# Retention attention and a top-2 adapter mixture: 64-token steps on 64x64 array tiles, an undecayed state, and a fixed order on every engine

## The chip, the cores and the metric

The kernel runs on one core of a Trainium2 chip. The metric is device time in microseconds (us): the median of the runs of one kernel. A core has a matrix engine (TensorE, PE in the profile; its weight loads are PEld), a vector engine (VectorE, DVE), a scalar engine (ScalarE, ACT), GpSimd (POOL), and SyncE (SP), which here only issues DMAs. Each engine works through its own queue in order; engines wait for one another by semaphores. PE writes to PSUM, which has eight banks; DVE and ACT copy out of PSUM.

## The reference, cut to what matters

```python
# q, k, v: [8 batches, 8 heads, 576 tokens, 64], float32
scores = scale * q @ k.T                       # per batch and head
ret    = scores * gamma[h] ** (i - j)          # for i >= j, else 0
x      = ret @ v                               # as [4608 tokens, 512]
logits = x @ w_gate                            # 8 experts, the best 2 are kept
w      = softmax(the two logits)
out    = x + sum over the two experts of w * ((x @ A[e]) @ B[e])   # rank 16
```

Because the decay is a product, `gamma ** (i - j)`, it can be split into a factor on q and a factor on v. Attention over earlier tokens can then go through a 64x64 state per head, the sum of k times v, instead of through scores.

## The kernel before, in words

The 576 tokens are cut into four blocks of 128 and one of 64. A unit is one block of two sequences (all 8 heads of both); there are 16 full units and 4 units for the last 64 tokens, in the order block by block, 20 in all. Inputs come by quads: four sequences of one block, three DMAs of 1 MB (q, k, v) on SP's queue, three quads of buffers. `issue(t // 2 + 2)` in the main loop asks for the quad that is two ahead.

For a unit t the stages are:

- `stage_T` (L229): PE transposes q and k by 64-row pieces, DVE copies q out while multiplying by the decay (`aqp`), ACT copies k out.
- `stage_S` (L291): scores k x q of 128 by 128 tokens per head, two 64-row tiles of the array side by side; DVE masks them into `rt` (L302).
- `stage_O`: the state's part of the output, `px` (L359), the new state's sum `pu` (L373); DVE adds (L387) and POOL multiplies by `g128`, the decay over 128 tokens (L388).
- `stage_R` (L408): masked scores times v, added in `px`; ACT copies `px` to `xT` (L417).
- `stage_Z` (L447): gate and all A matrices in one matmul per 128 rows, `pz`; then the routing on DVE and ACT (L460 to L479).
- `stage_B` (L512), `stage_X` (L493) and `stage_Y` (L533) of unit t - 1: x transposed back into `po`, the weighted z transposed, times B added in `po`; ACT copies `po` to `osb` (L543) and SP stores it (L548).

`scale_v` multiplies v by its decay on POOL (L197). Each float32 matmul shows as two matmuls and two weight loads in the profile; transposes show as one. The last four units (L341, L426, and the 64*64 form of L291) work on 64 tokens and use 64x64 tiles.

The order of instructions on each engine is set by the Tile framework's scheduler from the order of the code and the dependencies; PSUM comes from a pool of eight one-bank buffers that go around. SP's queue holds all loads and all stores of the kernel.

Of the kernel before, what the change touches and what calls it, by code (L numbers as in the profile page):

```python
# [9 lines left out]
FP32 = mybir.dt.float32  # L11
# [3 lines left out]
AFT = mybir.ActivationFunctionType  # L15


@with_exitstack
def kernel(
# [19 lines left out]
    LH = S - 128 * NFULL  # L39
    QUAD = 4  # L40
    NQ = B // QUAD

    scale = 1.0 / float(np.sqrt(Dh))
    gam = 1.0 - 2.0 ** (-5.0 - np.arange(H, dtype=np.float64))
    jj = np.arange(128, dtype=np.float64)

    ident32_np = np.eye(128, dtype=np.float32)
    tri_np = (jj[None, :] >= jj[:, None]).astype(np.float32)
    j64 = np.arange(128) % 64
    i64 = np.arange(64)  # L50
    trih_np = (i64[None, :] >= j64[:, None]).astype(np.float32)
    aqp_np = np.zeros((128, HP, 128), dtype=np.float32)
    g128_np = np.zeros((128, HP), dtype=np.float32)
    for hp in range(HP):
        for ho in range(2):
            g = gam[2 * hp + ho]
            aqp_np[64 * ho : 64 * ho + 64, hp, :] = scale * g ** jj[None, :]
            g128_np[64 * ho : 64 * ho + 64, hp] = g**128.0
    gv_np = np.stack([gam[h] ** (-jj) for h in range(H)], axis=1).astype(np.float32)
    gvh_np = np.stack([gam[h] ** (-j64.astype(np.float64)) for h in range(H)], axis=1).astype(  # L60
        np.float32
    )
    i64_np = np.concatenate([np.eye(64), np.eye(64)], axis=0).astype(np.float32)
    first_np = i64_np
    rest_np = np.concatenate(
        [ident32_np, tri_np, trih_np, gv_np, gvh_np, g128_np], axis=1
    ).astype(np.float32)
    NPK = rest_np.shape[1]
    dr_first = nc.inline_tensor(first_np, "c_first")
    dr_rest = nc.inline_tensor(rest_np, "c_rest")  # L70
    dr_aqp = nc.inline_tensor(aqp_np, "c_aqp")

    cpool = ctx.enter_context(tc.tile_pool(name="consts", bufs=1))
    iop = ctx.enter_context(tc.tile_pool(name="io", bufs=3))
    wk = ctx.enter_context(tc.tile_pool(name="work", bufs=2))
    mo = ctx.enter_context(tc.tile_pool(name="moe", bufs=3))
    pp = ctx.enter_context(tc.tile_pool(name="pp", bufs=8, space=bass.MemoryType.PSUM))

    id64 = cpool.tile([128, 64], FP32, tag="id64", name="id64")
    nc.sync.dma_start(out=id64, in_=dr_first.ap())  # L80
# [3 lines left out]
    pack = cpool.tile([128, NPK], FP32, tag="pack", name="pack")  # L84
    aqp = cpool.tile([128, HP, 128], FP32, tag="aqp", name="aqp")
    ident32 = pack[:, 0:128]
    tri = pack[:, 128:256]
    trih = pack[:, 256:320]
    gv = pack[:, 320 : 320 + H]
    gvh = pack[:, 320 + H : 320 + 2 * H]  # L90
    g128 = pack[:, 320 + 2 * H : 320 + 2 * H + HP]

    AW = []
    for par in range(2):
        AW.append(cpool.tile([128, HP, ER + E], FP32, tag=f"AW{par}", name=f"AW{par}"))
    Bcat = cpool.tile([128, Dm], FP16, tag="Bcat", name="Bcat")
    ident16 = cpool.tile([128, 128], FP16, tag="ident16", name="ident16")

    def load_moe():
        for dt in range(HP):  # L100
            nc.sync.dma_start(  # L101
                out=AW[0][:, dt, 0:ER].rearrange("p (e r) -> p e r", e=E),
                in_=moe_A[:, 128 * dt : 128 * dt + 128, :].rearrange("e d r -> d e r"),
            )
        nc.sync.dma_start(
            out=AW[0][:, :, ER : ER + E],
            in_=moe_w_gate.rearrange("(t p) e -> p t e", p=128),
        )
        nc.gpsimd.dma_start(out=Bcat, in_=moe_B.rearrange("e r d -> (e r) d"))


    nat = {}

    def issue_full(c, qd, split):
        tiles = []
        for src, tag in ((q, "q32"), (k, "k32"), (v, "v32")):
            tiles.append((src, iop.tile([128, QUAD * H, Dh], FP32, tag=tag, name=tag)))
        parts = ((0, 2), (2, 4)) if split else ((0, 4),)
        for lo, hi in parts:
            for src, tl in tiles:  # L120
                if split and lo == 0 and src is k:
                    nc.sync.dma_start(out=aqp, in_=dr_aqp.ap())
                if split and lo == 0 and src is v:
                    nc.sync.dma_start(out=pack, in_=dr_rest.ap())
                if split and lo == 2 and src is q:
                    load_moe()
                nc.sync.dma_start(  # L127
                    out=tl[:, lo * H : hi * H, :],
                    in_=src[
                        QUAD * qd + lo : QUAD * qd + hi, :, 128 * c : 128 * c + 128, :  # L130
                    ].rearrange("b h j d -> j (b h) d"),
                )
        for half in range(2):
            nat[(c, 2 * qd + half)] = [
                tl[:, half * 2 * H : half * 2 * H + 2 * H, :] for _, tl in tiles
            ]

    def issue_half(qd):

        s0 = 128 * NFULL  # L140
        tiles = []
        for src, tag in ((q, "q32"), (k, "k32"), (v, "v32")):
            tiles.append((src, iop.tile([128, QUAD * H, Dh], FP32, tag=tag, name=tag)))
        for slot in range(2):
            for src, tl in tiles:
                for par in range(2):
                    b = QUAD * qd + 2 * slot + par
                    nc.sync.dma_start(
                        out=tl[64 * par : 64 * par + LH, slot * H : slot * H + H, :],
                        in_=src[b, :, s0 : s0 + LH, :].rearrange("h j d -> j h d"),  # L150
                    )
            nat[(NFULL, 2 * qd + slot)] = [
                tl[:, slot * H : slot * H + H, :] for _, tl in tiles
            ]

    quads = [(c, qd) for c in range(NFULL + 1) for qd in range(NQ)]

    def issue(n):
        if n < len(quads):
            c, qd = quads[n]  # L160
            if c < NFULL:
                issue_full(c, qd, n == 0)
            else:
                issue_half(qd)

    issue(0)

    issue(1)
    nc.vector.tensor_copy(out=ident16, in_=ident32)
    gdec = cpool.tile([128, HP, 2, Dh], FP32, tag="gdec", name="gdec")  # L170
    nc.gpsimd.tensor_copy(
        out=gdec.rearrange("p a b d -> p a (b d)"),
        in_=g128.unsqueeze(2).broadcast_to((128, HP, 2 * Dh)),
    )
    P = [
        cpool.tile([128, HP, 2, Dh], FP32, tag=f"P{bp}", name=f"P{bp}")
        for bp in range(NP)
    ]

    def swap_aw():  # L180
        for ho in range(2):
            nc.gpsimd.tensor_copy(
                out=AW[1][64 * ho : 64 * ho + 64],
                in_=AW[0][64 - 64 * ho : 128 - 64 * ho],
            )

    units = [(c, 2 * qd + s) for c, qd in quads for s in range(2)]
    st = {}

    def scale_v(t):  # L190
        c, bp = units[t]
        full = c < NFULL
        v32 = nat[(c, bp)][2]
        nb = 2 if full else 1
        g = gv if full else gvh
        for b in range(nb):
            nc.gpsimd.tensor_tensor(  # L197
                out=v32[:, b * H : b * H + H, :],
                in0=v32[:, b * H : b * H + H, :],
                in1=g.unsqueeze(2).broadcast_to((128, H, Dh)),  # L200
                op=ALU.mult,
            )

    def stage_T(t):
        c, bp = units[t]
        full = c < NFULL
        q32, k32, v32 = nat[(c, bp)]
        qT = wk.tile([128, HP, 2, 128], FP32, tag="qT", name="qT")
        kT = wk.tile([128, HP, 2, 128], FP32, tag="kT", name="kT")
        L = 128 if full else LH  # L210
        for src, dst, nm in ((q32, qT, "q"), (k32, kT, "k")):
            dv = dst.rearrange("p a b i -> p a (b i)")[:, :, 0 : 2 * L].rearrange(
                "p a (b i) -> p a b i", i=L
            )
            if full:
                ps = [
                    pp.tile([128, HP, 2, 64], FP32, tag="pb", name=f"pt_{nm}")
                    for _ in range(2)
                ]
            else:  # L220
                ps = [
                    pp.tile([128, HP, 64], FP32, tag="pb", name=f"pt_{nm}")
                    for _ in range(2)
                ]
            for hp in range(HP):
                for b in range(2 if full else 1):
                    for r in range(2):
                        sl = slice(64 * r, 64 * r + 64)
                        nc.tensor.matmul(  # L229
# [381 lines left out]
```

## Time and profile before

| | |
|---|---|
| median of 3 runs | 208.59 us (207.39 to 208.97) |
| span of the profiled execution | 205.1 us |
| what lies around the span (median minus span) | 3.5 us |
| busy: PE, PEld, DVE, ACT, POOL | 183.8, 166.2, 108.7, 76.6, 59.6 us |
| granted TensorE clock | 0.995 mean |
| moved by DMA | 39.14 MB, mean 191 GB/s |

The profiled execution has no time of its own beside its span; the 3.5 us are the median of the runs less that span. The page's busy times say how long an engine had something running. The timeline says in which order, and a bracket at the end of a line tells how long the engine was idle before and what ended it. SPq is SP's own queue: a DMA's line there is the time that the issue held the queue, not the time of the transfer.

### The profile page before, as it was taken

The numbers are of one execution on the slowest core, as the hardware profiler recorded it, in microseconds if no ns is written. First come the engines' busy times: TensorE is split into PE (matmuls) and PEld (weight loads), VectorE is DVE, ScalarE is ACT, GpSimd is POOL, SyncE is SP. The second block draws the span as 40 slices with busy tenths as digits, with TensorE's granted clock in tenths as the row PEclk, the third lists the DMA queues.
The fourth block names the chain that finished last, engine by engine and source line by source line (L and its number), as shares of the span: only waits on it lengthen the run. The fifth ranks groups of instructions, "written<-read, shape, count | busy, mean of one in ns | idle before, by whom it ended". The sixth has DMA issues, their size and how long they took to land.

```text
span 205.1 us, 8039 instructions
## 1 busy us (share of the span) xinstructions
PE 183.8 (90%) x3564; PEld 166.2 (81%) x3564; DVE 108.7 (53%) x286; ACT 76.6 (37%) x206; POOL 59.6 (29%) x60
## 2 busy tenths in 40 slices
PE   0476989799999999999999999999999999999950
PEld 0376969598999999999999999999999899888830
DVE  0226364937374746465656565656565655456630
ACT  2022324153525262625252525253434344454430
POOL 1144323521818202727202720643222402000000
PEclk9999999999999999999999999999999999999997
DMA  5989999799998988991799969756545311222222
GB/s 114 277 109 246 249 243 280 194 290 290 253 319 245 261 249 274 284 297 36 220 286 254 266 215 293 213 145 179 150 118 158 96 51 60 101 79 76 58 47 61
DMA packets 57442, 39.14 MB, mean 191 GB/s; under 512 B 30912, under 2 KB 52672, under 8 KB 57408
## 3 DMA queue, kind: packets, MB, share of 16 engines
q1 hardware_dynamic: 57264, 38.50, 68.0%
q8 instruction: 28, 0.46, 0.9%
q0 software_dynamic: 144, 0.13, 0.4%
q14 instruction: 6, 0.05, 0.1%
HBM read 29.32 MB, written 9.44 MB: 189 GB/s over the span
## 4 chain that ended last, share of the span: by engine, by line
PE 72%; SPq 9%; DVE 7%; DMA 5%; ACT 3%; issue 1%; ACTq 0%
PE pz L447 16%; PE px L408 12%; PE ps_s L291 12%; PE pu L373 6%; PE px L359 6%; PE pt_q L229 5%; DMA k<-in_k_dram 5%; PE po L512 4%; SPq L127 4%; PE pt_k L229 4%; PE po L533 3%; DVE rt L302 2%; PE px L426 2%; ACT osb L543 2%; SPq L101 2%; PE pzt L493 2%
## 5 line engine op out<-in xcount | busy, mean ns | idle before, releaser
L197 POOL TENSOR_TENSOR v<-v,pack 128x512 f32<-128x512 f32 x36 | 36.6, 1042 | 28.0 <-DMA v<-in_v_dram 28.0
L417 ACT COPY xT<-px 128x512 f32<-128x512 f32 x32 | 18.7, 585 | 66.0 <-PE px L408 66.0
L388 POOL TENSOR_TENSOR P<-pn,gdec 128x512 f32<-128x512 f32 x16 | 20.3, 1271 | 75.3 <-DVE pn L387 58.9
L302 DVE TENSOR_TENSOR rt<-ps_s,pack 128x512 f32<-128x512 f32 x64 | 39.7, 682 | 4.2 <-PE ps_s L291 4.2
L291 PE MATMUL ps_s<-qT,kT 64*128 64x128 f32 (+1 forms) x640 | 37.4, 275 | 1.2 <-ACT kT L250 1.2
L447 PE MATMUL pz<-AW,xT 128*128 128x136 f32 x288 | 37.8, 283 | 0.4 <-ACT zT L498 0.4
L291 PEld LDWEIGHTS ps_s<-qT,kT 64*128 64x128 f32 (+1 forms) x640 | 33.7, 184 | 5.3 <-DVE lg L460 3.4
L241 DVE TENSOR_TENSOR qT<-pt_q,aqp 128x512 f32<-128x512 f32 x32 | 20.6, 686 | 31.1 <-PE pt_q L229 31.1
L408 PE MATMUL px<-rt,v 128*64 128x128 f32 x512 | 34.1, 275 | 1.8 <-DVE rt L302 1.7
L447 PEld LDWEIGHTS pz<-AW,xT 128*128 128x128 f32 x288 | 34.7, 190 | 0.6 <-ACT zT L498 0.5
L543 ACT COPY osb<-po 128x256 f32<-128x256 f32 x72 | 23.1, 375 | 25.8 <-PE po L533 25.8
L408 PEld LDWEIGHTS px<-rt,v 128*64 128x64 f32 x512 | 29.0, 137 | 3.8 <-DVE rt L302 2.5
L250 ACT COPY kT<-pt_k 128x512 f32<-128x512 f32 x32 | 17.2, 589 | 19.2 <-PE pt_k L229 19.2
L460 DVE COPY lg<-pz 128x16 f32<-128x16 f32 (+1 forms) x20 | 3.5, 173 | 35.0 <-PE pz L447 35.0
L229 PE MATMUL pt_q<-id,q 64*128 64x64 f32 x288 | 13.6, 234 | 6.7 <-DMA q<-in_q_dram 6.7
L373 PE MATMUL pu<-v,k 128*64 128x64 f32 x512 | 18.9, 225 | 0.0
L373 PEld LDWEIGHTS pu<-v,k 128*64 128x64 f32 x512 | 16.5, 137 | 2.7 <-issue 2.1
L229 PEld LDWEIGHTS pt_q<-id,q 64*128 64x128 f32 x288 | 10.8, 142 | 9.6 <-issue 9.4
L229 PE MATMUL pt_k<-id,k 64*128 64x64 f32 x288 | 12.8, 228 | 3.4 <-DMA k<-in_k_dram 3.4
L473 DVE SCALAR_TENSOR_TENSOR cm<-lg,m,sg 128x8 f32<-128x8 f32 x36 | 9.9, 294 | 8.8 <-ACT sg L468 8.8
L229 PEld LDWEIGHTS pt_k<-id,k 64*128 64x128 f32 x288 | 10.9, 143 | 3.8 <-issue 1.7
L359 PE MATMUL px<-qT,P 64*64 64x128 f32 x384 | 13.2, 275 | 0.0
(34 smaller groups left out, 139.9 us busy)
## 6 DMA issues: line engine op xcount, KB each, us to landing
out_dram<-osb SPq DMA_DIRECT2D x32, 256.0 KB, 3.2
q<-in_q_dram SPq DMA_DIRECT2D x2, 512.0 KB, 5.0
k<-in_k_dram SPq DMA_DIRECT2D x2, 512.0 KB, 6.0
v<-in_v_dram SPq DMA_DIRECT2D x2, 512.0 KB, 5.4
q<-in_q_dram SPq DMA_DIRECT2D x8, 128.0 KB, 3.4
k<-in_k_dram SPq DMA_DIRECT2D x8, 128.0 KB, 3.3
v<-in_v_dram SPq DMA_DIRECT2D x8, 128.0 KB, 4.1
out_dram<-osb SPq DMA_DIRECT2D x8, 128.0 KB, 2.4
```

The costliest lines, as they stand in the source:

```text
L197: nc.gpsimd.tensor_tensor(out=v32[:, b * H : b * H + H, :], in0=v32[:, b * H : b * H + H, :], in1=g.unsqueeze(2).broadcast_to((128, H, Dh) ...
L229: nc.tensor.matmul(ps[r][:, hp, b, :] if full else ps[r][:, hp, :], lhsT=src[sl, b * H + 2 * hp : b * H + 2 * hp + 2, :], rhs=id64[sl, :], ...
L241: nc.vector.tensor_tensor(out=o, in0=ps[r], in1=aqp[:, :, 64 * r : 64 * r + 64] .unsqueeze(2) .broadcast_to((128, HP, 2, 64)), op=ALU.mult,)
L291: nc.tensor.matmul(o, lhsT=kT[sl, hp, b, :], rhs=qT[sl, hp, b, :], start=(a == 0 and (b == 0 or not full)), stop=True, skip_group_check=True,)
L302: nc.vector.tensor_tensor(out=r.rearrange("p a b i -> p (a b) i"), in0=ps[ho].rearrange("p a b i -> p (a b) i"), in1=tri.unsqueeze(1).broa ...
L359: nc.tensor.matmul(px[b][64 * cc : 64 * cc + 64, hp, :], lhsT=P[bp][64 * ho : 64 * ho + 64, hp, b, :], rhs=qT[64 * ho : 64 * ho + 64, hp, ...
L373: nc.tensor.matmul(pu[64 * ho : 64 * ho + 64, hp, b, :], lhsT=s["k"][:, b * H + h, :], rhs=s["v"][:, b * H + h, :], start=(hp == 0 and b = ...
L388: nc.gpsimd.tensor_tensor(out=pf, in0=pn, in1=gdec.rearrange("p a b d -> p (a b d)"), op=ALU.mult,)
L408: nc.tensor.matmul(px[b][64 * cc : 64 * cc + 64, hp, :], lhsT=s["v"][:, b * H + h, :], rhs=rt[h][:, b, :], start=(c == 0 and hp == 0), sto ...
L417: nc.scalar.copy(out=xt, in_=px[b])
L447: nc.tensor.matmul(pz[:, b, :], lhsT=xts[b][:, dt, :], rhs=AW[b][:, dt, :], start=(dt == 0), stop=(dt == HP - 1), skip_group_check=True,)
L543: nc.scalar.copy(out=osb[:, b, :, cc ^ b, :], in_=po[cc][:, b])
```

## The change

All attention goes in steps of 64 tokens. A unit is still 128 rows of two sequences, but the 128 rows are two steps g = 0, 1 of 64 tokens (for the last 64 tokens: two pairs of sequences, so there are 2 such units in place of 4, and 18 units in all). Scores, state products, state sums and scores times v are all 64x64x64 matmuls on the four 64x64 tiles of the array, so the upper right 64 by 64 part of each 128 by 128 block of scores is not computed, and there are more and smaller matmuls. q and v are multiplied by the whole decay from the sequence's start (`gq`, `gv`, by position) on POOL before they are used, so the state is a plain sum: two DVE adds for each unit, no decay of the state. ACT copies both transposes out of PSUM.

`tc.manual_schedule()` keeps the order of the code on every engine. Banks are named by hand. The code keeps the two row tiles of the array from writing into one bank at once: where the state products change over, PE's next matmul waits for a NOP on SP's queue, which itself waits for PE's last matmul (`end_turn`, `begin_turn`). Two changeovers come in each row of the main loop. Stores are issued at the end of a row, two rows after the unit's attention. Inputs have four quads of buffers instead of three. The constants come in one small DMA; A and the gate come by 12 DMAs on SP's queue instead of 5, B by 4 on POOL's instead of 1.

The core of the diff (the new side; the old functions stand above):

```diff
+    def scale(t, which, eng):
+        c, _ = units[t]
+        x = nat[units[t]][0 if which == "q" else 2].rearrange("p (s h) d -> p s h d", s=2)
+        tab = gq if which == "q" else gv
+        for s in range(2):
+            eng.tensor_tensor(out=x[:, s], in0=x[:, s],
+                in1=tab[:, c, :].unsqueeze(2).broadcast_to((128, H, Dh)), op=ALU.mult)
...
+    def bankA(r):
+        return (2, 3) if r % 2 == 0 else (6, 7)
...
+    def pe_S(t):
+        ps = [bank(ho, [128, HP, 2, 64], name=f"ps_s{ho}") for ho in range(2)]
+        for hp in range(HP):
+            for s in range(2):
+                for ho in range(2):
+                    for g in range(2):
+                        nc.tensor.matmul(
+                            ps[ho][half(g), hp, s, :],
+                            lhsT=kT[half(ho), g, hp, s, :],
+                            rhs=qT[half(ho), g, hp, s, :],
...
+    def end_turn(ins):
+        n = nc.sync.nop(nofuse=True)
+        tc.add_manual_dep(n.ins, ins.ins.name, SYNC, reason="row tile's last write")
+        turn.append(n)
+
+    def begin_turn(ins):
+        if turn:
+            tc.add_manual_dep(ins.ins, turn.pop().ins.name, SYNC, reason="other row tile's bank")
+
+    def pe_I(t, part):
+        for a in range(HP // 2):
+            for s in range(2):
+                for par in range(2):
+                    g = part ^ par
+                    P = state_of(t, s, g)
+                    if P is None:
+                        continue
+                    hp = 2 * a + par
+                    for ho in range(2):
+                        c = ho ^ par
+                        ins = nc.tensor.matmul(
+                            px[g][half(c), hp, s, :],
+                            lhsT=P[0][half(ho), hp, P[1], :],
+                            rhs=qT[half(ho), g, hp, s, :],
...
+                        begin_turn(ins)
+        end_turn(ins)
...
+    def pe_U(t, part):
+        for hp in range(2 * part, 2 * part + 2):
+            for s in range(2):
+                for g in range(2):
+                    for ho in range(2):
+                        h = s * H + 2 * hp + ho
+                        nc.tensor.matmul(pu[g][half(ho), hp, s, :],
+                            lhsT=k32[half(g), h, :], rhs=v32[half(g), h, :], ...
...
+    def ev_U(t):
+        if P0 is None:
+            nc.vector.tensor_copy(out=f(Pm), in_=f(pu[0]))
+        else:
+            nc.vector.tensor_tensor(out=f(Pm), in0=f(pu[0]), in1=f(P0), op=ALU.add)
+        nc.vector.tensor_tensor(out=f(Pn), in0=f(pu[1]), in1=f(Pm), op=ALU.add)
...
+    def pe_R(t):
+        for hp in range(HP):
+            for s in range(2):
+                for g in range(2):
+                    for ho in range(2):
+                        c = ho ^ (hp & 1)
+                        ins = nc.tensor.matmul(px[g][half(c), hp, s, :],
+                            lhsT=v32[half(g), s * H + 2 * hp + ho, :],
+                            rhs=rt[ho][half(g), hp, s, :], ...
+                        begin_turn(ins)
...
+    for r in range(NU + 2):
+        if r % 2 == 0:
+            issue(r // 2 + 2)
+        if r + 2 < NU:
+            scale(r + 2, "q", nc.gpsimd)
+            scale(r + 2, "v", nc.gpsimd)
+        if r + 1 < NU:
+            pe_T(r + 1, "q")
+            ev_T(r + 1, "q")
+            pe_T(r + 1, "k")
+        if 0 <= r - 2:
+            pe_B(r - 2)
+        free = bankA(r + 1)
+        if 0 <= r - 2:
+            pe_pzt(r - 2, free[0])
+        if r + 1 < NU:
+            ev_T(r + 1, "k")
+        if 0 <= r - 1 < NU:
+            pe_Z(r - 1, free[1])
+            route1(r - 1)
+        if 0 <= r - 2:
+            pe_Y(r - 2)
+            ev_Y(r - 2)
+        if 0 <= r - 1 < NU:
+            route_sig(r - 1)
+        if r < NU:
+            pe_S(r)
+            ev_S(r)
+            alloc_x(r)
+            pe_I(r, 0)
+            pe_U(r + 1, 0)
+            pe_I(r, 1)
+            pe_U(r + 1, 1)
+        if 0 <= r - 1 < NU:
+            route2(r - 1)
+        if r < NU:
+            ev_U(r + 1)
+            pe_R(r)
+            ev_x(r)
+        if 0 <= r - 2:
+            store(r - 2)
```

Before this loop the new code calls `issue(0)` (a quad in halves, with the weights' DMAs between them) and `issue(1)`, and transposes unit 0 and sums its state (`pe_T(0, ...)`, `pe_U(0, ...)`). `pe_T`, `pe_B`, `pe_pzt`, `pe_Z`, `route1`, `route2`, `pe_Y` do what stages T, B, X, Z and Y did, on the same shapes. The 1 MB loads of a quad have the same access patterns as before.

## The prediction

> **What bounds the kernel now.** I read the page first, then the chain of waits, then the timeline of PE and of SP's queue. The page has PE busy for nine tenths of the span and no other engine above 53%.
>
> ```profile
> PE 183.8 (90%) x3564; PEld 166.2 (81%) x3564; DVE 108.7 (53%) x286; ACT 76.6 (37%) x206; POOL 59.6 (29%) x60
> PEclk9999999999999999999999999999999999999997
> DMA  5989999799998988991799969756545311222222
> ```
>
> From about 51 us the chain is PE alone and repeats every 10.05 us, once a unit. PE's timeline of one unit (start, length):
>
> ```profile
> 103.36 2.07 PE L447 MATMUL pz<-AW,xT 128*128 128x136 f32 x16
> 105.27 0.60 PE L533 MATMUL po<-Bcat,zT 128*128 128x256 f16 x4
> 105.80 2.06 PE L291 MATMUL ps_s<-qT,kT 64*128 64x128 f32 x32
> 107.78 1.10 PE L359 MATMUL px<-qT,P 64*64 64x128 f32 x32
> 108.81 1.15 PE L373 MATMUL pu<-v,k 128*64 128x64 f32 x32
> 109.80 1.92 PE L408 MATMUL px<-rt,v 128*64 128x128 f32 x32
> 111.65 0.52 PE L229 MATMUL pt_q<-id,q 64*128 64x64 f32 x10
> ```
>
> Groups overlap at their ends, so I take starts less starts. The chain of waits has the same pieces without the overlap: pt_q 0.64, pt_k 0.49, po 0.49, pzt and its gap 0.22, pz 1.91, po 0.44 (together 4.19), scores 1.99, state products 1.03, state sums 1.08, scores times v 1.75: 10.04 us.
>
> The start is another stage. In 41.8 us PE finishes only three units (some 31 us of work) because inputs arrive slowly, and SP's own queue shows how: one 1 MB load holds it for as long as the data ahead of it needs to drain.
>
> ```profile
> 29.11 3.54 SPq L127 DMA_DIRECT2D q<-in_q_dram  x1
> 33.11 4.74 SPq L127 DMA_DIRECT2D k<-in_k_dram  x1
> 38.30 3.52 SPq L127 DMA_DIRECT2D v<-in_v_dram  x1
> 41.92 3.69 SPq L548 DMA_DIRECT2D out_dram<-osb  x1
> ```
>
> Later, with DMAs quiet beforehand, two stores and a quad still hold the queue from 97.26 to 107.59, **10.3 us**:
>
> ```profile
> 97.26 0.93 SPq L548 DMA_DIRECT2D out_dram<-osb  x2
> 98.40 0.72 SPq L127 DMA_DIRECT2D q<-in_q_dram  x1
> 99.58 3.50 SPq L127 DMA_DIRECT2D k<-in_k_dram  x1
> 103.54 4.05 SPq L127 DMA_DIRECT2D v<-in_v_dram  x1
> ```
>
> Today nobody but the DMAs themselves waits for that queue. After the change PE does.
>
> **The change, part by part: matmuls.** The price of a 64x64x64 matmul is in the last units, which have that shape now:
>
> ```profile
> 181.69 0.69 PE L291 MATMUL ps_s<-qT,kT 64*64 64x64 f32 x32
> 182.20 1.11 PE L341 MATMUL pq<-qT,P 64*64 64x64 f32 x32
> 183.39 1.12 PE L426 MATMUL px<-rh,v 64*64 64x64 f32 x32
> ```
>
> L291 uses all four tiles in turn: 182.20 less 181.69 is 0.51 us for 32 records, 16 ns each. L426 also uses four; once its inputs are there its records go four every 58 ns, 14.6 each. L341 visits only two tiles and pays 32. In the new code scores, state products, sums and scores times v each visit four tiles in turn and have 64 records a unit, so each costs 64 x 15.5 = 1.0 us (0.94 to 1.02; 2.0 if state products behaved like L341). A row costs 4.19 + 4.0 = **8.2 us** for 10.04: 1.0 saved on scores, 0.75 on scores times v, 0.1 on sums, nothing on state products. The 4.19 stay, shapes being the same. There are 18 rows for 20 units.
>
> The Trainium skill, "TensorE: Matmul & The Clock Gate", section "Wait — 56ns, not 53.3ns?", has a floor of about 25 ns between starts, however small the matmul. That speaks against this change: 256 records would be 6.4 us for 4.0, and a row would be longer than today's. The 14.6 and 16 ns rows say the floor does not hold across tiles, and I go by them.
>
> **Other engines.** DVE loses the q copies (20.6 + 3.0 us) and nearly half of the mask (64 to 36 of 682 ns, 19 us) and gains 16 state adds of 0.69 (11 us): about 77 for 108.7 us. ACT gains the q copies, 36 x 0.585 = 21 us, and has about 6.1 us in a row of 8.2. POOL has 70 products of 1.04, 4.2 us a row. These are hidden behind PE. If not, one place shows first: U's first half writes the bank that ACT empties with four osb copies (two take 0.65, so 1.3) after Y, with only scores and half the state products (1.5 us) and 0.2 of handoffs between: 0.2 us late (0 to 0.4), in 8 rows not held otherwise: 1.6 us. Removing POOL's state decay (20.3 us) gains nothing, since PE did not wait for it.
>
> **SP's queue.** The NOPs stand, in program order, behind every DMA issued before them. Moved past or onto that queue: a quad in every even row stands ahead of both its NOPs, a unit's stores behind them.
>
> - *Start.* Row 0 comes after issue(0), issue(1) and issue(2). Before, the third quad's v leaves the queue at 41.8 us. The constants shrink from 458 to 106 KB (1.4 us at 250 GB/s), while the weights cost 12 issues for 5 (5.4 us now; 12 x 0.58, the shortest, is 7.0: 1.6 more if not covered by draining). I take 40.5 us (39 to 42.5) for the first matmul of the second half of row 0's state products. Before, three units were done at that time.
> - *Even rows 4 to 10.* Count from the last state product of the row before. SP sees it 0.3 us later, passes two stores and a quad (10.3), and wakes PE (0.1): 10.7. PE meanwhile has half the sums 0.5, scores times v 1.0, 4.19, scores 1.0, half the products 0.5 and half the sums 0.5, with 0.2 of bank wait: 7.8. PE waits 2.9 us (2.0 to 3.6) four times. Row 2 has no stores ahead: 1.9. Together **13.5**. Rows 12 and 14 load half quads (the first quad's halves held the queue 4.95 us): none.
> - Behind the waiting NOP stand stores and next loads; loads are two rows ahead, osb has four buffers, so nothing waits for those. Behind the waiting matmul stands all of PE.
> - *Handoff.* No row has a PE to SP to PE trip. A semaphore event on SP takes 17 to 28 ns, a matmul 218 from its start to its end: at least 0.25 us, and by DVE to PE handoffs (0.2 to 0.5 idle) at most 0.6. I take 0.45, covered by 0.5 us of sums, except in rows 15 to 17, which have none: twice 0.45 each.
>
> **Start of the clock.** PE's first score group took 3.79 us where the next took 2.06, and the granted clock is down again after the end:
>
> ```profile
> 199.00:202.00 3.00, 0.39 (x2) 0.11 (x2) 0.00 (x0) 0.76 (x3) 0.00 (x0) 1.00 0.55 124
> 202.00:205.00 3.00, 0.00 (x0) 0.00 (x0) 0.00 (x0) 0.00 (x0) 0.00 (x0) 0.65 0.20 46
> ```
>
> The last column but two is the clock; it drops to half at 202.87, 3.3 us after the last matmul. PE idles well over 10 us in row 0, so it restarts at half speed: 1.8 us (3.79 less 2.06, rounded up). The 2.9 us waits are just below 3.3 and I price them at nothing (at most 1.8 each). The same skill page, section "Part 1: The HAM clock gate", gives the idle window as about 3.4 us; by it the sum would be the same.
>
> **The end.** From the last unit's pz to the end are now 9.4 us (195.68 to 205.06). A whole unit adds the px copies 1.35 ahead, 0.75 of pz, 0.65 of routing and transposed z, 0.65 of the other unit's osb copies in front of its sigmoids, 0.65 of its own, 1.1 for four stores: 14.6, with handoffs 15.0.
>
> **Sum:** 40.5 to row 0's second half; 2.0 for the rest of row 0; row 1 7.5 (no B and Y; 0.45 for its first xT); rows 2 to 14 13 x 8.2 = 106.6 and 1.6; rows 15, 16 8.1 each and row 17 7.9 (24.1); waits 13.5; end 15.0; clock 1.8. That is **212.6 us** of span against 205.1. The median before lies 3.5 above its span, so 216.1: PE saves 1.85 us in each full unit and two short units, and SP's queue takes it back, some 18 us at the start (unit 2's scores times v end at 60.1, now at 41.7) and 11.6 in rows 4 to 10.
>
> **Rivals.**
>
> - *PE is not held by SP's queue* (the NOPs pass ahead of loads, so the fixed order isn't what it says). For it: only code order, no row, puts them behind. Against: every store in SP's timeline stands behind loads until they leave. Data then set the start: row 3 cannot begin before the third quad's k, about 43.5. Then 12 x 8.4 = 100.8, 24.1, 15.0: 183.4, **186.9** with 3.5. It decides if two stores and a quad pass in under 7.8 us. 0.14.
> - *Only the start is held.* A quad's issue takes 0.7 per load when the queue has drained (q at 98.40), and pauses of PE may let it. Against it are 3.50 and 4.05 right after. 212.6 less 13.5 plus 3.5: **202.6**. 0.14.
> - *The waits drop the clock.* 2.9 grows past 3.3 and five restarts cost 1.8 each: 216.1 + 9 = **225.1**. 0.13.
> - *State products at 32 ns*, like L341: 1.0 in each of 17 rows, half of it hidden in five: 216.1 + 14 = **230**. Against: four tiles, not two. 0.04.
>
> **Numbers.** My forecast gets 0.55, at 216.1; with the bounds above (start, waits, bank wait, handoffs) 207 to 224. A change under 1% cannot be told from none here. Faster by over 1% (below 206.5): the first rival and most of the second, 0.27. Within 1%: the low end of mine and the rest of the second, 0.07. Slower: 0.66. The range 198 to 228 leaves out the first rival and the top of the last two, under 0.2.
>
> **What would show it.** In the profile after: PE's four attention groups near 1.0 us each, PE's busy time well below 183.8; PE idle from before 30 to about 40 us, ended by SP; in rows 2 to 10 every second state-product group preceded by about 2.9 us of idle ended by SP's queue, the other rows near 8.2. It is wrong if PE's waits end on DVE, ACT or a DMA, if state products in even rows start without a wait, or if a 64x64 group takes over 1.3 us.

## The result and the profile after

The changed kernel takes **271.0 us** (median of 4 runs, 266.66 to 273.95); the kernel before took 207.99 us beside it. The ratio is **1.2908** [1.2792, 1.3023]: 29% slower, where 3.6% (216.1 us) was forecast, and far above the range's 228. Medians are over all runs and ratios over undisturbed ones alone, so the two need not divide to the same figure, and the profiled execution, from which the rows below come, is one of the slower ones. It took 271.86 us, its span is 269.9, its mean granted clock 0.873 (0.995 before).

The page first, with the lines that answer to those shown of the kernel before, then the shares of the chain that ended last and the costliest groups:

```profile
PE 177.7 (66%) x5612; PEld 161.9 (60%) x5612; DVE 77.1 (29%) x197; ACT 91.4 (34%) x236; POOL 74.7 (28%) x81
PEclk9999755799799869985998589977999999899995
DMA  8959999919836990789179807990494197022215
...
q8 instruction: 44, 0.72, 1.2%
...
PE 45%; SPq 36%; issue 12%; DVE 2%; ACT 2%; ACTq 0%
...
L406 PE MATMUL px<-qT,Pm 64*64 64x64 f32 x512 | 26.3, 240 | 27.7 <-SPq L385 26.8
...
L432 PE MATMUL pu<-v,k 64*64 64x64 f32 x1024 | 29.8, 248 | 10.4 <-issue 6.2
...
L466 PE MATMUL px<-rt,v 64*64 64x64 f32 x1152 | 28.0, 247 | 11.1 <-issue 10.2
...
L336 PE MATMUL ps_s<-qT,kT 64*64 64x64 f32 x1152 | 23.4, 228 | 5.2 <-issue 5.2
```

PE was busy 90% of the time and is now busy 66%; the other engines are nowhere near full. PE's idle time has two names. `SPq L385` is the NOP of the handoff, which was forecast. `issue` is time in which PE waited for nothing that the profile shows, and that was not forecast. The clock row, nearly flat before, has holes all along the span. Line q8 looks harmless at 1.2% of the DMA engines, but it is the one that matters: 44 packets of kind "instruction". The page of before has 28:

```profile
q8 instruction: 28, 0.46, 0.9%
```

The chain of waits (start, length) shows the start, one row without an SP wait, an even row with one, and a piece of the odd row behind it:

```profile
43.17 4.29 SPq L139
47.57 1.00 PE px L406 x13
...
64.90 0.72 PE ps_s L336 x34
65.62 2.03 issue
67.65 0.80 PE ps_s L336 x25
...
84.58 3.85 SPq L139
88.89 5.21 SPq L139
94.21 1.13 PE px L406 x32
...
102.93 1.09 PE ps_s L336 x64
104.02 0.48 PE px L406 x31
104.50 0.55 PE pu L432 x30
105.22 1.31 issue
```

PE waits for SP until 47.57, as the third quad's v leaves SP's queue (43.17 plus 4.29). At 102.93 the groups have the price that was forecast: 64 records of scores in 1.09 us, half the state products in 0.48. But then PE stands still for 1.31 us, and at 65.62 in the middle of one scores group for 2.03 us, with its inputs there. The group after that stop, 25 records in 0.80 us, runs at half the pace: the granted clock is at half from 67.96 to 71.37.

SP's queue (start, length) over the same stretch:

```profile
20.96 2.34 SPq L139 DMA_DIRECT2D q<-in_q_dram  x1
...
38.44 4.28 SPq L139 DMA_DIRECT2D k<-in_k_dram  x1
43.17 4.29 SPq L139 DMA_DIRECT2D v<-in_v_dram  x1
71.11 12.08 SPq L319 DMA_DIRECT2D out_dram<-osb  x4
83.42 0.70 SPq L139 DMA_DIRECT2D q<-in_q_dram  x1
84.58 3.85 SPq L139 DMA_DIRECT2D k<-in_k_dram  x1
88.89 5.21 SPq L139 DMA_DIRECT2D v<-in_v_dram  x1
```

The two quads that row 0 has to wait for hold the queue from 20.96 to 47.46, 26.5 us (23.4 before). Ahead of them the 12 loads of A and the gate held it from 6.24 to 16.36, 10.1 us.

**Whose are the stops?** From here on a gap is counted from the start of one matmul to the start of the next, which is some 0.2 us more than the idle time in a profile row. After 50 us PE has 24 gaps of over 1 us. Four end on SP, at 94.21, 120.33, 147.47 and 174.75. The other 20 resume, when all that stands in PE's queue is counted (weight loads, matmuls, and 121 semaphore and drain instructions), at instructions 1217, 1473, 1985, 2753, 3521, 3777, 4289, 5057 and so on to 9665: every difference is a multiple of 256. Each of the 20 ends 1.2 to 1.8 us after a packet of 16,384 bytes on queue q8 has landed; the four on SP end 4.8 us or more after one. PE's 11,224 matmuls and weight loads divided by 256 are 43.8, and 44 packets came; before, 7,128 are 27.8, and 28 came. So a packet holds 256 instructions of 64 bytes, and the theory for the experiments was: **PE runs out of instructions.** In the expectations that theory is called F; Q is the theory of the prediction, that SP's queue holds PE and the rest is cheap.

### The profile page after: what moved, and what is told of

Its sections match the earlier page's. It is cut to its first block, busy times and chain, and to the rows that moved or that the text cites. A ratio compares the mean times of both kernels' runs of the same rounds, so it can differ in the third digit from the quotient of the medians.

```text
span 269.9 us, 12185 instructions
## 1 busy us (share of the span) xinstructions
PE 177.7 (66%) x5612; PEld 161.9 (60%) x5612; DVE 77.1 (29%) x197; ACT 91.4 (34%) x236; POOL 74.7 (28%) x81
## 4 chain that ended last, share of the span: by engine, by line
PE 45%; SPq 36%; issue 12%; DVE 2%; ACT 2%; ACTq 0%
SPq L139 25%; PE pz L240 10%; PE px L466 8%; PE px L406 6%; PE pu L432 5%; PE ps_s L336 5%; SPq L129 3%; PE pt_q L191 3%; SPq L99 3%; PE pt_k L191 3%; PE po L213 2%; SPq L149 2%; PE po L294 2%; SPq L319 2%; DVE rt L350 1%
## 5 line engine op out<-in xcount | busy, mean ns | idle before, releaser
L160 POOL TENSOR_TENSOR q<-q,pack 128x512 f32<-128x512 f32 x34 | 34.7, 1042 | 84.3 <-DMA q<-in_q_dram 70.1
L406 PE MATMUL px<-qT,Pm 64*64 64x64 f32 x512 | 26.3, 240 | 27.7 <-SPq L385 26.8
L406 PEld LDWEIGHTS px<-qT,Pm 64*64 64x64 f32 x512 | 22.1, 151 | 31.3 <-SPq L385 28.0
L432 PE MATMUL pu<-v,k 64*64 64x64 f32 x1024 | 29.8, 248 | 10.4 <-issue 6.2
L466 PE MATMUL px<-rt,v 64*64 64x64 f32 x1152 | 28.0, 247 | 11.1 <-issue 10.2
L466 PEld LDWEIGHTS px<-rt,v 64*64 64x64 f32 x1152 | 24.9, 159 | 12.6 <-issue 12.0
L432 PEld LDWEIGHTS pu<-v,k 64*64 64x64 f32 x1024 | 25.5, 158 | 11.7 <-issue 6.8
L336 PE MATMUL ps_s<-qT,kT 64*64 64x64 f32 x1152 | 23.4, 228 | 5.2 <-issue 5.2
L406 PE MATMUL px<-qT,P 64*64 64x64 f32 x512 | 21.4, 231 | 7.5 <-issue 7.3
L336 PEld LDWEIGHTS ps_s<-qT,kT 64*64 64x64 f32 x1152 | 20.3, 140 | 9.4 <-issue 5.9
L191 PEld LDWEIGHTS pt_q<-pack,q 64*128 64x128 f32 x288 | 12.6, 160 | 19.0 <-DVE q L160 7.6
```

What stands on the lines that cost most here:

```text
L160: eng.tensor_tensor(out=x[:, s], in0=x[:, s], in1=tab[:, c, :].unsqueeze(2).broadcast_to((128, H, Dh)), op=ALU.mult,)
L191: nc.tensor.matmul(ps[g][:, hp, s, :], lhsT=src[half(g), s, 2 * hp : 2 * hp + 2, :], rhs=id64[half(g), :], is_transpose=True, start=True, ...
L336: nc.tensor.matmul(ps[ho][half(g), hp, s, :], lhsT=kT[half(ho), g, hp, s, :], rhs=qT[half(ho), g, hp, s, :], start=True, stop=True, skip_g ...
L406: ins = nc.tensor.matmul(px[g][half(c), hp, s, :], lhsT=P[0][half(ho), hp, P[1], :], rhs=qT[half(ho), g, hp, s, :], start=x_start(t, g, c) ...
L432: nc.tensor.matmul(pu[g][half(ho), hp, s, :], lhsT=k32[half(g), h, :], rhs=v32[half(g), h, :], start=True, stop=True, skip_group_check=True,)
L466: ins = nc.tensor.matmul(px[g][half(c), hp, s, :], lhsT=v32[half(g), s * H + 2 * hp + ho, :], rhs=rt[ho][half(g), hp, s, :], start=x_start ...
```

## The experiments

Eight kernels ran. The first three test F against Q, the next two test single steps of the forecast, the last three ask what in the kernel before could be had.

**The handoff on ScalarE's queue, which holds no DMA.** In the changed kernel:

```diff
-        n = nc.sync.nop(nofuse=True)
+        n = nc.scalar.nop(nofuse=True)
```

> The changed kernel with the two NOPs of each row on ScalarE's queue in place of SyncE's; nothing else differs. Theory Q (SyncE's queue alone holds PE, and the extra time over the forecast is more of the same): no wait on SyncE is left, rows are 8.2 us, and the time is near 187 us, the figure of the first rival in the prediction. Theory F (PE runs out of instructions: it has 11,224 of them against 7,128, and 64x64 matmuls use up 256 in 2 us, faster than the next 256 arrive): the idle of 1.3 to 2.8 us with no releaser ('issue') stays, once every 256 or 512 PE instructions, some 25 times, 2 us each; then 215 to 230 us. Theory C (the clock halves after SyncE's waits and is what makes the rest slow): clock back at 0.99 and no 'issue' idle, near 190 us.

Measured: 254.81 us, 1.2077 [1.1923, 1.2231] times the kernel before; the profiled execution has a span of 248.2 us and a clock of 0.932. PE's waits:

```profile
PE px L466 <- issue: 17.2, 11, 3.4
PE pu L432 <- issue: 8.2, 5, 2.9
...
PE px L406 <- issue: 6.8, 4, 2.6
```

(The columns are us in total, times, longest.) No wait for a handoff is left among them. Of the 29% lost, 8 points went with SP's queue: some 17 of 60 us. Theory Q alone falls, and so does C: the stops are there, and the clock did not come back to 0.99. F is right in kind, and all 20 gaps of over 1 us after 45 us resume at the first instruction of a packet, but its figure of 215 to 230 us was low. The gaps grew to 3.6 us while the loads came earlier; that the loads lengthened them fits the streams below and was not tested here.

**Only the first two quads loaded, and used for all rows,** which makes the DMAs quiet:

```diff
+        if n >= 2:
+            for half in range(2 if c < NFULL else 1):
+                nat[(c, 2 * qd + half if c < NFULL else qd)] = nat[(0, 2 * (n % 2) + half)]
+            return
...
-        c, _ = units[t]
+        c = 0
```

> The changed kernel with the NOPs where they are, but only the first two quads are loaded; later rows use these again (their output is therefore not attention over the later tokens). SyncE issues no loads in the loop, stores remain, and DMA traffic is light after 35 us. Theory Q: waits on SyncE stay only at row 0, ending near 34 us (the second quad's last load leaves SyncE then), rows 8.2 us, near 34 + 155 = 189 us span. Theory F: 'issue' idle remains though the DMA engines are idle, some 25 to 30 times at 256-instruction distances, 1.3 to 2.5 us each: 225 to 240 us. If the idle shrinks below 1 us with the quiet DMA engines, it was load on the DMA engines that made the fetch late.

Measured in one run: 222.18 us (F said 225 to 240, Q 189), span 220.4, clock 0.958. PE's waits, and then a piece of the chain with two whole rows:

```profile
PE px L470 <- issue: 10.4, 9, 1.8
...
PE px L410 <- SPq L389: 4.8, 1, 4.8
PE pu L436 <- issue: 4.3, 4, 1.3
```

The chain:

```profile
80.68 1.09 PE ps_s L340 x64
...
83.68 0.93 PE px L470 x63
...
84.94 1.17 issue
...
90.21 1.09 PE ps_s L340 x64
...
93.15 1.22 issue
...
99.88 0.20 PE ps_s L340
```

SP holds PE once, in row 0, and no later load is there to hold anything. These two rows take 9.5 and 9.7 us (90.21 less 80.68, 99.88 less 90.21), 1.3 to 1.5 above the 8.2 of the forecast, and one stop of 1.2 us stands in each, at full clock (38.1 to 106.4). From row 1's scores to row 17's a row takes 10.1 us on average. All 16 gaps of over 1 us after 45 us resume at the first instruction of a packet. So the stops need no loads, and with every load after the start taken away the kernel is still slower than before.

**PE alone on constant data:** streams of 128x128 matmuls, of 64x64x64 on four tiles (s0q, s1q), of 64x64 by 128 (m), then 128x128 and 64x64x64 again (s0d, s1d) while twelve 1 MB loads and then stores run.

```diff
+    wide(192, "a")
+    small(768, "q")
+    mid(512)
+    last = wide(96, "b")
...
+    small(768, "d")
```

> No attention and no mixture: PE alone runs streams of float32 matmuls on constant data, and zeros are stored. In order: 192 matmuls of 128x128 by 128 (384 records); 768 of 64x64 by 64 on four tiles (1536 records, 3072 PE instructions with weight loads); 512 of 64x64 by 128 (1024 records); then, while 12 MB of loads run, 96 of 128x128 and 768 of 64x64 by 64. Theory F: the 64x64 by 64 stream stops every 256 PE instructions, also without DMA traffic; 128 records take 2 us of work and 1.5 to 2.5 us of idle, 28 to 36 ns per record over the stream; the 64x64 by 128 stream (32 ns a record, 4.1 us for 256 instructions) has idle under 1 us per 256 or none; the 128x128 stream none; with loads running the stops are longer. Theory Q or C (nothing about instructions): both 64x64 streams run at their own 15.5 and 32 ns with no stops, 24 us for the first in all.

The groups (busy, mean ns of one, then the idle time before them):

```profile
L50 PE MATMUL w_a<-a 128*128 128x128 f32 x576 | 67.5, 282 | 1.2 <-DVE a L42 1.2
...
L68 PE MATMUL s1d<-a 64*64 64x64 f32 x768 | 32.2, 254 | 25.0 <-issue 25.0
...
L59 PE MATMUL m<-a 64*64 64x128 f32 x1024 | 29.5, 270 | 0.7 <-issue 0.5
...
L68 PE MATMUL s1q<-a 64*64 64x64 f32 x768 | 25.1, 219 | 17.3 <-issue 17.3
```

The s0 and s1 records run at once, so 1536 of them take busy plus idle of one line: 42.4 us quiet, **27.6 ns a record**, though inside a block they start 14 to 15 ns apart. With DMAs it is 57.2 us, **37.2 ns**. A record brings its weight load, so 256 instructions are 128 records: **3.5 us quiet, 4.8 us with loads**. Under the loads the clock was at half for 21.5 of the 57.2 us, so the 4.8 may not be the loads' doing alone. The stream by 128 needs 30.2 us for 1024 records, 3.8 us for 256 instructions, and has next to no stops (0.55 us from start to start at most); the 128x128 stream has none. The quiet stops resume at instructions 1217, 1473, 1729, 1985 and on by 256, at the same numbers as in the changed kernel, though there is no attention here. They last 1.16 to 2.13 us quiet and 1.4 to 4.6 us with loads. The quiet streams differ in the size of their matmuls, and so in the rate at which they use up instructions; that the stops keep to every 256th instruction speaks for the rate. F stands.

These two rates give a bound that needs no trace, an estimate from the runs above: the changed kernel has 11,224/18 = 624 PE instructions a row, 2.44 packets, so a row cannot be shorter than 8.6 us quiet or 11.6 us under load. On average the rows took 10.1 in the run with two quads and 12.3 in the changed kernel, SP's waits included. A full unit of the kernel before has 396, 1.55 packets or at most 7.4 us, under its 10.05, and its trace has no stop of over 1 us for instructions.

**One SP handoff a unit, in the kernel before,** from the last score matmul to the first of scores times v:

```diff
+        n = nc.sync.nop(nofuse=True)
+        tc.add_manual_dep(n.ins, ins.ins.name, SYNC, reason="scores done")
+        turn.append(n)
```

> The kernel before with one part of the change alone: in every unit a NOP on SyncE's queue waits for the last score matmul, and the first matmul of scores times v waits for that NOP. PE instructions stay 7,128, so theory F has no stops here. Theory Q by the prediction's terms: the first unit's scores times v cannot start until the third quad's v leaves SyncE's queue, 41.9 us in place of 16.5 (18 to 22 us lost at the start); later 12.1 us pass on PE from one handoff to the next in even units, more than the 10.6 that two stores and a quad hold the queue, so no or small waits; 226 to 232 us in all. If SyncE's queue holds PE for longer than its issues show, waits of 3 us and more come in every second unit and the time is above 245.

Measured in one run: 229.07 us, span 227.0. The wait, the last load ahead of it on SP's queue, and PE's timeline:

```profile
PE px L418 <- SPq L322: 23.8, 1, 23.8
```

SP's queue:

```profile
36.44 3.34 SPq L127 DMA_DIRECT2D v<-in_v_dram  x1
```

PE:

```profile
39.99 2.40 PE L418 MATMUL px<-rt,v 128*64 128x128 f32 x20 [23.80 <-SPq L322]
```

One wait of 24 us at the start, ended as the third quad's v leaves the queue at 39.78, and none after it: the cost is 21 us, inside the 226 to 232 us expected. So a handoff through the queue of the loads costs about what the forecast's start says (18 us), with no small matmuls in play.

**Scores and state products of the kernel before cut into two of 64 columns,** to bring in instructions without the handoff:

```diff
-                                lhsT=P[bp][64 * ho : 64 * ho + 64, hp, b, :],
-                                rhs=qT[64 * ho : 64 * ho + 64, hp, b, :],
+                                lhsT=P[bp][64 * ho : 64 * ho + 64, hp, b, :],
+                                rhs=qT[64 * ho : 64 * ho + 64, hp, b, js],
```

> The kernel before with more instructions for the same array work: each score matmul and each state-product matmul of a full unit is cut into two of 64 moving columns (scores stay on 64x128 tiles, 64 records at 31 ns for 32 at 62; state products 64 at 15.5 for 32 at 32). A full unit has 528 PE instructions for 400, the same work of 10.05 us, no tile of a new shape in the scores, and SyncE's queue as before. Theory F: scores and state products together are 256 instructions in 3 us, less than the 3.5 us that the quiet stream showed for 256; so PE idle with no releaser of about 0.5 to 1.5 us appears in many units, at distances of a multiple of 256 PE instructions: 5 to 15 us in all, 213 to 223 us. If the stops of the changed kernel came from the 64x64 scores, the handoffs or the clock, there are none here and the time stays at 208 us within 2.

Measured: 232.12 us, 1.1232 [1.1165, 1.13]. Its timeline:

```profile
107.60 3.79 PE L289 MATMUL ps_s<-qT,kT 64*128 64x64 f32 x64
111.32 1.16 PE L368 MATMUL px<-qT,P 64*64 64x64 f32 x64
```

It does not test F: scores of 64 columns on a 64x128 tile cost 58 ns a record (3.72 us for 64), not the 31 that I took from transposes of that shape, so the unit became longer by array time, 256 instructions took some 4.8 us, and only two gaps of about 1 us appeared, both at the start of a packet. The state products, 64 records in 1.1 us for 32 in 1.03, cost the same array time cut or uncut, as the forecast had it.

**Only the causal half of the scores, in the kernel before,** on 64x64 tiles, with the mask in two pieces:

```diff
+                        for kb in range(2):
...
+                                    ps[ho][64 * kb : 64 * kb + 64, a, b, 64 * kb :],
+                                    lhsT=kT[sl, hp, b, 64 * kb : 64 * kb + 64],
+                                    rhs=qT[sl, hp, b, 64 * kb :],
```

> The kernel before, with one part of the change alone: the scores of a full unit by 64x64 tiles without the upper right quarter (per head and sequence one 64x64 by 128 and one 64x64 by 64 in place of one 64x128 by 128), the mask in two DVE operations, its zero quarter kept in fixed buffers. From the rows: 32 records at 32 ns and 32 at 15.5 are 1.52 us for 1.99, so 0.47 us in each of 16 units, 7.5 us less: about 201 us. Theory F agrees: a unit has 464 PE instructions for 400, one fetch per 5 us, so no 'issue' idle. If 64x64 tiles were themselves the trouble (a changeover between tile shapes), scores would stay near 2 us or the groups around them would grow, and the time stays at 208 us or above.

Measured: 209.04 us, 1.0014 [0.996, 1.0068]; no difference. From a unit's scores to its state sums PE takes 2.77 us for 3.02, so the saving is 0.25 us a unit (0.1 in the first block, which has no state products), some 3.5 us, and not the 7.5 expected. And the mask became 128 DVE instructions of 405 ns (43.5 us busy) for 64 of 682 (39.7), and PE's weight loads wait longer for it. In this run:

```profile
PEld px L428 <- DVE rt L320: 6.9, 19, 0.5
```

In the kernel before:

```profile
PEld px L408 <- DVE rt L302: 2.5, 8, 0.4
```

Units without such a wait come 9.92 us apart (10.04 before), others 10.1 to 11.8. So the expected 201 us was wrong on both sides: the saving on PE was half of what I took, and I had not costed the mask. That the mask takes all of the rest back is read from this one trace and was not tested.

**The second quad of the kernel before in six loads of 512 KB instead of three of 1 MB:**

```diff
-                issue_full(c, qd, n == 0)
+                issue_full(c, qd, n < 2, n == 0)
```

> The kernel before, with the second quad loaded in halves (six DMAs of 512 KB, the first unit's q, k, v before the second unit's) in place of three DMAs of 1 MB. In the kernel before, unit 2 waits for v of the whole quad: POOL's product starts at 34.3 us, its state sums at 36.2, while its own half of the data is about half of 3 MB, some 6 us, earlier. If data for unit 2 set the start, PE reaches its steady row of 10.05 us 5 to 8 us earlier and the time is 201 to 204 us. If the start is set by the whole amount of data (the third quad then comes no earlier), PE waits for the third quad instead and the time stays within 2 us of 208.

Measured: 206.25 against 207.9 us, 0.9897 [0.9856, 0.9937]: **1.0% less**. The interval lies below 1, but the gain is under the 2% from which a kernel is called faster here, and short of the 201 to 204 us expected. The fifth unit's transposes start at 48.56 us for 51.46, only 2.9 us earlier: the units ahead of it come 9.67 us apart (the masks start at 34.84 and 44.51), because DVE gets to the mask only behind the routing of the unit before. And of these 2.9 us only 0.3 are left in the last unit, as two later units, 10.84 and 11.46 us long, wait for the mask again. Both are read from the timelines of one execution and were not tested:

```profile
34.84 2.47 DVE L302 TENSOR_TENSOR rt<-ps_s,pack 128x512 f32<-128x512 f32 x4
...
44.12 0.48 DVE L479 TENSOR_TENSOR zc<-pz,cm 128x128 f16<-128x128 f32 x2
44.51 2.47 DVE L302 TENSOR_TENSOR rt<-ps_s,pack 128x512 f32<-128x512 f32 x4
```

**The same, with the loads of A and the gate behind the first quad:**

```diff
-                if first and lo == 2 and src is q:
-                    load_moe()
...
+        if first:
+            load_moe()
```

> The kernel before with the second quad in halves (as in the run before) and the weights' five DMAs moved behind the first quad's second half. Unit 1's k came at 20.1 us because 4.5 us of small weight transfers ran ahead of it; without them unit 1's scores can start some 4 us earlier, if the weights (needed by unit 0's gate matmul, which stands ahead of those scores on PE) come by 19 us. Expected 1 to 3 us less than with the halves alone, 203 to 205 us. If the gate matmul now waits for the weights, nothing is gained: 206 us.

Measured, on another chip than the run before, with runs of the kernel before beside it: 206.68 against 206.09 us, 1.0024 [0.9985, 1.0064]: the gain is gone, as expected for the case that the gate waits for its weights. Its first matmul does, for 1.73 us, to 21.64, and the clock is at half from 23.4 to 26.8. That these two take the gain was not tested.

## Why the prediction was wrong, by its own steps

- **Price of the 64x64 matmuls: right as array time.** 1.0 us a group was forecast (0.94 to 1.02); 1.09, 2 x 0.48, about 2 x 0.5 and 0.93 came where no stop fell in. The rival that state products cost 32 ns falls.
- **Row of 8.2 us: the step that failed.** It added array times and took for granted that PE always has its next instruction. The terms of the sum put row 1's scores at 47.8 (40.5, 2.0, the clock's 1.8, and 3.5 of row 1's 7.5) and have 146.1 us from there to row 17's scores; the trace has 196.8 (54.35 to 251.2). PE's four waits for SP in that stretch (2.21, 3.35, 2.62, 1.54, from start to start) sum to 9.7. Its 35 other gaps of over 0.3 us sum to 45.3. Of these, 28 resume at the first instruction of a packet and sum to 42.8; the other 7, 2.6 us, are short waits of 0.3 to 0.4 us between engines, such as the forecast allowed for. So there are about **43 us of missing instructions**, a term that the sum did not have. I had the row that shows it: 28 packets of kind "instruction" stand on the page of before. The 14.6 and 16 ns were read from groups of 32 records, 64 instructions, too short to use up a packet.
- **The floor of 25 ns** that the Trainium skill gives ("TensorE: Matmul & The Clock Gate", "Wait — 56ns, not 53.3ns?") was set aside for the rows of 14.6 and 16 ns. The runs show 14 to 15 ns inside a block, under that floor, and 27.6 ns over a long stream, just above it. By that page's floor a row would have been an estimated 10.6 us, nearer to the 12.3 measured than my 8.2, though the runs show a supply of instructions and not a floor for each.
- **SP's queue holds PE: right; its size at the start: too low.** Row 0's second half came at 47.57 for 40.5 (39 to 42.5). The 12 loads of A and the gate took 10.1 us where I allowed 5.4 to 7.0, and the two quads 26.5 for 23.4. By row 1's scores that is 6.6 us (54.35 for 47.8). The rivals that SP holds PE nowhere, or only at the start, are out.
- **Even rows: right in place, near in size by luck.** Rows 4, 6, 8 and 10 wait for SP, 1.54 to 3.35 us, sum 9.7, where 2.9 (2.0 to 3.6) each was forecast. But both sides of that difference were too small: from the last state product of the row before, SP took 12.6 to 13.1 us to wake PE where 10.7 was forecast, and PE, held up by its stops, was there after 10.0 to 11.7 where 7.8 was; rows 12 and 14 don't wait, as forecast. A bare handoff, priced at 0.45 us, took 0.30 to 0.34 in rows 12 and 15 to 17. Row 2 has stops of 2.25 and 1.59 us for lack of instructions and no wait for SP, where 1.9 was forecast: PE arrived late anyway. Moving the handoff gave back 17 us, the start and the waits together.
- **The clock: too low, and the rival half right.** I priced waits under 3.3 us at nothing. The clock was at half for 41.0 us between 51 and 235 us. What is left of the 50.7 us that the rows lost, 50.7 + 13.5 - 9.7 - 42.8, is some 11.7 us: 0.29 us for each us at half speed. It is a remainder and was not measured alone. The rival "the waits drop the clock" had the mechanism, not the cause: of its seven drops between 51 and 235 us two fall into an SP wait (119.16, 146.46), two come where a stop and an SP wait stand close together (91.85, 177.18), and three come with a stop alone. The window of about 3.4 us of the same page ("Part 1: The HAM clock gate") was no safe bound here: a lone stop of 2.25 us, ending at 67.65, was followed by half clock at 68.0. The length of a stop does not decide by itself. In all ten traces the clock changes only on a grid of 3.41 us (in the changed kernel at 27.00, 30.41, 50.89, 67.96, 71.37 and on). At full clock, every piece of that grid in which a matmul record was running for less than 0.42 of the time was followed by half clock, and none with more than 0.55; between the two both came.
- **The end and the other engines: right.** From row 17's scores to the end 18.7 us were forecast and 18.7 came; DVE is busy 77.1 us for 77 forecast, and neither DVE nor ACT nor POOL sets a row: from row 1's scores to row 17's PE's waits for them are under 0.5 us each.

Together: 6.6 at the start, 42.8 of stops and the remainder of 11.7 for the clock, less 3.8 in SP's waits, are the 57 us between the span of 212.6 and that of 269.9. This counts where PE stood, and not what each would save alone: on the chain itself issue has 12%, 33 us, and the other stops fell into rows that SP held anyway and only shortened SP's share.

Not tried: the changed kernel without any handoff, whose point is to keep the two row tiles of the array from writing one bank at once, and the same attention with fewer instructions for the same array time. Open is what decides over the clock between 0.42 and 0.55 of a piece of the grid: the quiet stream, with gaps of 2.13 us, kept full clock at 0.44, and the run with two quads, with gaps of 1.97 and 2.35 us, lost it at 0.49 and 0.48.

## What to carry to other kernels

Before cutting matmuls smaller, count PE's instructions, matmuls and weight loads alike, divide by 256, and hold the 3.5 us (quiet) to 4.8 us (under load) that the streams took for each against the array time of the stage: if it is longer, the supply of instructions sets the pace, and a pace read from a short group does not hold. Don't hand over from PE to PE through a queue that issues loads: one such wait in the first unit cost 21 us in an otherwise unchanged kernel. A saving on the busiest engine has to be priced on its neighbour too: causal scores saved some 3.5 us on PE, PE waited longer for the mask on DVE, and the kernel was no faster.

## What the runs showed of the hardware

- PE's instructions arrive in packets of 256, 16 KB each, on a DMA queue of their own. Dense 64x64x64 float32 matmuls use up 256 in 1.9 us (128 records, 14.8 ns from start to start), and PE then stops 1.2 to 2.1 us with quiet DMAs and up to 4.6 us under loads.
- The granted clock can halve after stops well under 3.3 us: after 2.25 us in the changed kernel and after 1.97 us, at 106.4, in the run with two quads. It changed only on a grid of 3.41 us.
- On a 64x128 tile a float32 matmul of 64 columns costs 58 ns a record, a transpose of the same shape 31 ns; cutting a 128-column matmul in two there doubled its time (1.99 to 3.72 us).
- On SP's queue, 11 of the 12 small loads of A and the gate held it 0.60 to 0.65 us each, one 2.69; with the pauses between them all twelve took 10.1 us.
